# Absolute decay factors and one causal mask in a retention kernel, parameters spread by matmuls, and another written-out order of its first half

## The chip, the cores and the metric

One core of one Trainium2 chip runs the whole program. The time is the device time of one execution, in microseconds; for the kernel before it is the median of three runs.

## The reference, cut to what matters

Three layers in a row. First a retention layer over q, k, v of shape (2, 8, 768, 64): a state of 64x64 per head decays by gamma at each position.

```python
gamma = 1.0 - 2.0 ** (-5.0 - np.arange(H, dtype=np.float32))
for t in range(S):
    state = gamma[None, :, None, None] * state + np.einsum('bhd,bhe->bhde', k[:, :, t], v[:, :, t])
    y[:, :, t] = scale * np.einsum('bhd,bhde->bhe', q[:, :, t], state)
```

Its output, as 1536 tokens of 512 features, passes two feed-forward layers of 2048 hidden units. The first has a rational function between its two products (parameters a, four numbers, and b, two numbers); the second has h * sigmoid(h).

```python
P = a[0] + a[1] * h + a[2] * h2 + a[3] * h3
Q = 1.0 + np.abs(b[0]) * np.abs(h) + np.abs(b[1]) * h2
g = P / (Q + 1e-06)
```

The weights of the feed-forward layers arrive as 64-bit floats.

## The kernel before, in words

**Retention by chunks.** The sequence is cut in 6 chunks of 128 positions for each of 2 batches: 12 chunks c0 to c11, chunk index ci = c // 2. The function `attention(c, ...)` loads four tiles of 256 KB each: qT and kT (features down the partitions), vn and kn (positions down the partitions); kn is missing for the last ci. TensorE makes the scores (`sc`, L458, 16 instructions, into two PSUM banks). VectorE multiplies them with a mask that holds the decay between two positions of one chunk (`am` tiles, two instructions, the 512 KB tile `msk`). kn is multiplied with gamma to the minus position (`gk`, in the small tile `cst`). From kn and vn TensorE makes what the state grows by (`grow`, L491, 16 instructions), and from vn and the masked scores, with the old state `bd` and the scaled q, the output (`outs`, L503 x16 and, from the second ci on, L513 x8). q is multiplied with gamma to the position (tile `gq`, one load of 256 KB for each ci above 0) after its scores are made, since the scores take it plain. ScalarE and VectorE split the output in a high and a low part (`xh`, `xl`), the operands of the feed-forward layer. The kn and q multiplications are VectorE's in chunks 0 to 3 and GpSimd's (POOL) after that. Chunks 0 to 3 make up the first group of 512 tokens, 4 to 7 the second.

**Feed-forward.** The weights come in pairs of 128-wide blocks; a use u of a pair has four raw loads of 512 KB ("in" 0 and 1, "out" 0 and 1). ScalarE (two ACTIVATEs) and VectorE (one instruction) turn a raw load into fp32, ScalarE makes the high part and POOL the low part (L414). A use has two steps; step s has an input product of 12 matmuls (L550, into PSUM bank h0 or h1 in the first 20 steps), some ten elementwise instructions of ScalarE and VectorE, a split in `gh` and `gl`, and four output products of 3 to 6 matmuls (L603, banks acc0 to acc3). The first two input products need chunks 0 to 3 and the weights of use 0; the third (step 2) needs use 1.

**Buffers that gate loads.** Three buffers each for qT, kn, vn and for raw weights, two for kT: the load of kT of c2 waits until the scores of c0 are made, and a raw load until the merge of the raw load three before it. All loads are issued by SyncE (SP), one queue, in order: a load that waits holds back those behind it.

**The order.** The program is a list of 2312 operations; the packed constant `ORDER` gives their places, and each engine runs its operations in that order. Nothing is moved at run time. Unpacked, SP's list begins like this (q0 is qT of chunk 0; u0.in1 the second "in" load of use 0; spill a store of converted weights):

```
q0 k'0 cst msk u0.out0 v0 k0 k'1 q1 k1 u0.in0 q2 k'2 v1 gq2 k'3 q3 u0.in1 v2 k2 k3 q4 k'4 v3 k4 gq4 a v4 k5
u0.out1 b u1.in0 u1.in1 spill q5 k'5 v5 u1.out0 k7 k6 spill k'6 q6 v6 gq6 ...     (k' is kT, k is kn)
```

and TensorE's:

```
warm-up, sc0, outs0, sc1, grow0, sc2, outs1, sc3, grow1, outs2, grow2, sc4, outs3, grow3, grow4, outs4,
step 1 in, step 0 in, sc5, grow5, outs5, sc6, grow6, outs6, step 2 in, sc7, step 0 out ...
```

The tile `par` holds the parameters; two loads spread a and b over the 128 partitions, VectorE negates a (L354), ScalarE takes the absolute values of b (L828, L829). A warm-up of 11 products of zeros (L837) runs at the start.

Of the kernel before, what the change touches and what calls it, by code (L numbers as in the profile page):

```python
# [23 lines left out]
R = {'lw': -463.92, 'T0': 689.59, 'tau0': 13.93, 'tau1': 122.19, 'c0': -129.63, 'dc': 67.51, 'conv': 39.61, 'half': 427.29, 'absl': -34.77, 'raw': 455.03, 'ret': 752.06, 'spl': -417.39, 'hi': 301.24, 'lo': 31.56, 'inn': -277.93, 'later': -32.81, 'split': -554.53, 'out': 359.39, 'evac': -363.13, 'qload': -20.08, 'scl': 238.79, 'sc': 858.37, 'am': -44.15, 'gr': 112.48, 'av': -547.62, 'bd': 198.47, 'xh': -201.14, 'xl': 110.32, 'glp': 48, 'lop1': 24, 'lop2': 30, 'scp': 4, 'ps': 17, 'ksc': 103.89, 'qa': -467.29, 'ka': 0, 'late': 20, 'mid': 4, 'pev': -317.29, 'pld': -385.01, 'cg': -489.85, 'wm': 11, 'mk': 26.43, 'ck': 21.3, 'g2': (1, 0, 2), 'ch0': 269.21, 'ch1': -102.81, 'ch2': 64.3, 'ch3': 22.33, 'ch4': -52.46, 'ch5': 5.42, 'ch6': -78.23, 'ch7': 237.84, 'ch8': 90.06, 'ch9': -61.88, 'ch10': -106.39, 'ch11': -212.52, 'ru0': 218.22, 'lu0': -107.8, 'ru1': 40.68, 'lu1': -106.06, 'ru2': 91.09, 'lu2': 146.01, 'ru3': -37.17, 'lu3': -39.51, 'rhalf': 125.38, 'wsum': 20.0, 'kd': 4, 'hb': 20}  # L24
# [7 lines left out]
    'c-jru0~-+L8UWDO@0VM)wrp!*aoNVQ?G_f6ZQHiBY}>Z6g{`{xSDfcWgQ$Q2a15fu50D5F0|P+>hzyY+BE*DP5F27ZTu2UaAPO9Z6L1oe!cIsJ=^',  # L32
    'zPYgM5%5_Cp592n8TBB!FG88<Ign_z_aT9!LpUAv<J&c(51ZLmEg6r=buOhF{<($OJjzAf$rSZ~$_^At(X`ArIt*BTyPj!Ou_@DuF;5s0(L7;Xh#',
    'f3(CVjI0NONG8~0^Pz*}Kc{m5TAU70+3Qz?qLRF{%-{310hZ68B7*vA`P!p=dcW_V)AovWP!waYlwV)0}#9q)E4nqrQ39X<5{D7z63S5J$fN1y<U',
    'PEN855GY}AZ!D@p%FBI#?S+P#*5GsuER~Z1x=tS+<<1#93o-B+i(Y7K@@xgZ{ZzWf|wWs+d@0I3+>?^+=urN0XxEF=medi8$`ngP!J1XEbIbZp*z',
    'IG_?Q4cKq2e{MG>$xI*x(gAu3LV;qW*71I6(n^n;HO9TQ_hOoYWS36{mASO)vTAMg|&!4pV_8L$LChJWER^oLLI1qMJl%#6QaGE9!YVtR~&m2e6S',
    'g&|NFdt+=Ih{Iqy6v0v$7b{>Dtc)ozBmRgrF$-43fshFYL00?;|AfIX60%_}tc}?*2j;}S*avgrAp8?YLp`j6^>GyZfpu{(4#$#M9v8znTnbgG8Z',
    'LopkP=70Sjdg3FfF#i*7zH?!8AAyQe#_ekNvR$HpKBT0XkqioCMWzD0ajV*a`DvUd)GiZ~)GLiZ~1>!$g<~jj%CJ#m+b$o8U;CfYWd~&W0}76}w?',
    'm?2a{X4lKu&xB^GvM4Sb)a0brA**FKAV>4`lbD<^n#Cfm=SK(Tmi}P?kF2Do08rR`uT#p-YBhH6ScnQZ~HCl)Zp*k&q8ng&D<3T)xNAWNo!{2ckj',
    'K=j)n^r;t+5nSq2=>Eu(2S<w7F>jv@d_Tn<5-94(kd8>jpzh6q!!eiuHy>0fmd-k)T5Jl3QuEWYDw4dCf>px*bA57VqA)=VFzx-C%6o6;~l(<XK*',  # L40
    'KO!<zIIpJRPm1NZP5zQC9G3fIC}tVQ?nH~NDA;lKD5zvDUFjpuPMKE#bMmUiKGoJo`EHNL@bxCh74J{(VP5$GKvy+@+WFo7=MMQla0XexccEzp|&',
# [93 lines left out]
def retention_two_mlps(  # L135
# [114 lines left out]


    cst = Buf("cst", [P, NGAM])
    msk = Buf("msk", [P, 2, HP, P])
    gk = cst.t[:].rearrange("p (c h) -> p c h", h=H)
    par = Buf("par", [P, 14])
    ab, na, b1, b0, lb = par.t[:, 0:6], par.t[:, 6:10], par.t[:, 10:11], par.t[:, 12:13], par.t[:, 13:14]
    cq = par.t[:, 11:12]
# [61 lines left out]
    def heads(t):  # L319
        return t[:].rearrange("p (a t) -> p a t", a=HP)  # L320
# [103 lines left out]
    def attention(c, s_banks, o_banks):  # L424
# [10 lines left out]
        kT, qT = load(0.0, kTs, kt[b, ci]), load(0.1, qTs, qt[b, ci])  # L435
        vn = load(0.3, vns, v[b, ci])
        kn = load(0.4, kns, k[b, ci]) if grows else None
        if grows:

            if c < R["ka"]:  # L440

# [498 lines left out]
```

## Time and profile before

| | us |
|---|---|
| three runs | 580.83, 581.77, 584.45 (median 581.77) |
| profiled execution, device time | 583.26 |
| its span, first to last instruction | 581.5 |
| TensorE busy in the span | 567.3 |
| VectorE, ScalarE, POOL busy | 427.6, 405.2, 174.2 |

The profiled execution lies 1.49 us above the median of the three runs; 1.76 us of it are outside the span. Busy times overlap; they add up to more than the span.

### The profile page before, as it was taken

How to read it: one execution, taken by the hardware profiler on the slowest of the kernel's cores; microseconds unless marked ns; L12 is line 12 of the kernel's file. 1: busy time of each engine (PE TensorE's matmuls, PEld its weight loads, DVE VectorE, ACT ScalarE, POOL GpSimd, SP SyncE). 2: the span in 40 equal slices, each digit the busy share in tenths (PEclk: the TensorE clock that was granted, in tenths of full speed). 3: DMA queues.
4: the chain of work that ended last, by engine and by line, in shares of the span. 5: the costliest groups of instructions: out<-in, count | busy, mean ns of one | idle time of the engine just before them, and what ended most of it. 6: DMA issues, size and time to landing. Idle time of an engine off the chain costs nothing.

```text
span 581.5 us, 8229 instructions
## 1 busy us (share of the span) xinstructions
PE 567.3 (98%) x2902; PEld 467.4 (80%) x2902; DVE 427.6 (74%) x673; ACT 405.2 (70%) x697; POOL 174.2 (30%) x141
## 2 busy tenths in 40 slices
PE   7879999999999999999999999999999999999997
PEld 6767777888888888888888888888888888888885
DVE  3878888798788887798878566578887888663331
ACT  2577988999988887787998888776634545334432
POOL 0435545534644523553463653310000000000000
PEclk8997999999999999999999999999999999999999
DMA  8999856443123310032044667865433422116811
GB/s 299 304 386 312 276 165 235 144 144 112 36 76 106 104 42 20 0 92 90 19 162 147 217 218 246 280 212 167 139 98 108 146 73 91 54 38 207 278 57 73
DMA packets 42585, 86.81 MB, mean 149 GB/s; under 512 B 4656, under 2 KB 4656, under 8 KB 42544
## 3 DMA queue, kind: packets, MB, share of 16 engines
q1 hardware_dynamic: 42544, 86.29, 44.5%
q8 instruction: 23, 0.38, 0.3%
q14 instruction: 18, 0.15, 0.1%
HBM read 65.30 MB, written 20.97 MB: 148 GB/s over the span
## 4 chain that ended last, share of the span: by engine, by line
PE 92%; DMA 3%; ACT 1%; issue 1%; DVE 1%; SPq 1%; POOL 1%; POOLq 0%; DVEq 0%; ACTq 0%
PE acc L603 45%; PE h L550 19%; PE a L550 10%; PE h L766 7%; PE a L766 7%; DMA raw<-in_moe_w_in_dram 2%; PE a L513 1%; DMA qT<-in_qt_dram 1%; PE a L503 1%; PE a L458 1%; SPq L362 1%; PE a L491 1%; PE acc L458 0%; POOL kn L336 0%; ACT wt L328 0%
## 5 line engine op out<-in xcount | busy, mean ns | idle before, releaser
L336 POOL TENSOR_TENSOR gl<-s,gh 128x512 fp32r<-128x512 f32 x48 | 62.7, 1307 | 111.6 <-ACT gh L328 74.8
L603 PE MATMUL acc<-gh,oh 128*128 128x512 f32 x192 | 75.8, 395 | 0.0
L603 PE MATMUL acc<-gl,oh 128*128 128x512 f32 x192 | 74.8, 390 | 0.0
L603 PE MATMUL acc<-gh,ol 128*128 128x512 f32 x192 | 74.8, 389 | 0.0
L603 PE MATMUL acc<-oh,gh 128*128 128x512 f32 x192 | 74.7, 389 | 0.0
L603 PE MATMUL acc<-oh,gl 128*128 128x512 f32 x192 | 74.7, 389 | 0.0
L603 PE MATMUL acc<-ol,gh 128*128 128x512 f32 x192 | 74.7, 389 | 0.0
L550 PE MATMUL h<-xh,ih 128*128 128x512 f32 x168 | 66.3, 395 | 0.0
L550 PE MATMUL h<-xh,il 128*128 128x512 f32 x168 | 65.7, 391 | 0.0
L550 PE MATMUL h<-xl,ih 128*128 128x512 f32 x168 | 65.7, 391 | 0.0
L414 POOL TENSOR_TENSOR il<-wt,ih 128x512 fp32r<-128x512 f32 x36 | 47.1, 1317 | 48.4 <-ACT ih L409 46.2
L343 DVE SCALAR_TENSOR_TENSOR wt<-wt,raw 128x512 int32<-128x512 int32 x64 | 46.2, 732 | 19.9 <-ACT raw L328 12.4
L414 POOL TENSOR_TENSOR ol<-wt,oh 128x512 fp32r<-128x512 f32 x36 | 47.6, 1325 | 29.0 <-ACT oh L409 24.5
L328 ACT ACTIVATE raw<-raw,par 128x512 int32<-128x512 uint32 x64 | 48.3, 759 | 6.1 <-DMA raw<-in_moe_w_in_dram 5.0
L343 DVE SCALAR_TENSOR_TENSOR s<-s,par,h 128x512 f32<-128x512 f32 x65 | 48.2, 744 | 1.2
L328 ACT ACTIVATE wt<-raw 128x512 f32<-128x512 f32 x64 | 42.2, 660 | 6.4 <-DMA raw<-in_moe_w_out_dram 4.0
L603 PEld LDWEIGHTS acc<-gh,oh 128*128 128x128 f32 x192 | 36.0, 188 | 7.8
L603 PEld LDWEIGHTS acc<-oh,gh 128*128 128x128 f32 x192 | 36.0, 188 | 7.5
L603 PEld LDWEIGHTS acc<-gl,oh 128*128 128x128 f32 x192 | 36.0, 188 | 7.5
L603 PEld LDWEIGHTS acc<-oh,gl 128*128 128x128 f32 x192 | 36.0, 188 | 7.5
L603 PEld LDWEIGHTS acc<-ol,gh 128*128 128x128 f32 x192 | 36.0, 188 | 7.4
L328 ACT ACTIVATE gh<-s 128x512 fp32r<-128x512 f32 x56 | 35.0, 626 | 9.9 <-PE acc L603 3.7
(249 smaller groups left out, 1292.0 us busy)
## 6 DMA issues: line engine op xcount, KB each, us to landing
raw<-in_moe_w_out_dram SPq DMA_DIRECT2D x32, 512.0 KB, 4.4
raw<-in_moe_w_in_dram SPq DMA_DIRECT2D x32, 512.0 KB, 4.7
spill<-wt SPq DMA_DIRECT2D x48, 256.0 KB, 4.7
wt<-spill SPq DMA_DIRECT2D x48, 256.0 KB, 2.9
qT<-in_qt_dram SPq DMA_DIRECT2D x12, 256.0 KB, 5.7
kT<-in_kt_dram SPq DMA_DIRECT2D x12, 256.0 KB, 5.9
vn<-in_v_dram SPq DMA_DIRECT2D x12, 256.0 KB, 5.9
kn<-in_k_dram SPq DMA_DIRECT2D x10, 256.0 KB, 6.1
```

What stands on the lines that cost most here:

```text
L328: lambda: nc.scalar.activation(out=out_, in_=in_, func=func, **kw),
L336: op(eng, dur, rank, lambda: e.tensor_tensor(out=out_, in0=in0, in1=in1, op=alu), reads, writes, port)
L343: lambda: nc.vector.scalar_tensor_tensor(out=out_, in0=in0, scalar=scalar, in1=in1, op0=op0, op1=op1),
L362: op("swdge" if swdge else "sync", us, rank, lambda: e.dma_start(out=out_, in_=in_), reads, writes)
L414: e.tensor_tensor(out=sl.t[nm + "l"][:, us], in0=wt.t, in1=sl.t[nm + "h"][:, us].bitcast(F32), op=ALU.subtract)
L458: nc.tensor.matmul(heads(sb_[j].t)[:, hp, :], kT.t[js, hp, :], qT.t[js, hp, :], start=True, stop=True)
L491: nc.tensor.matmul(st.t[j * D : (j + 1) * D, hp * D : (hp + 1) * D], kn.t[:, 2 * hp + j, :], vn.t[:, 2 * hp + j, :], start=(hp == 0), stop ...
L503: nc.tensor.matmul(heads(xo.t)[j * D : (j + 1) * D, hp, :], vn.t[:, 2 * hp + j, :], heads(am[j].t)[:, hp, :], start=(hp == 0), stop=not mo ...
L513: nc.tensor.matmul(heads(xo.t)[:, hp, :], old.t[:, hp, :], qT.t[:, hp, :], start=False, stop=True, skip_group_check=True,)
L550: nc.tensor.matmul(h.t, sl.t[w][:, ws], x[g].t[:, c, :], start=(n == 0), stop=(n == 3 * KD - 1))
L603: nc.tensor.matmul(a.t, a1, a2, start=(first and n == 0), stop=(last and n == 2))
L766: nc.tensor.matmul(b_.t, w[0](c, wlo), x[0](c, xlo), start=(start and n == 0), stop=(n == 5), skip_group_check=True)
```

## The change

- The mask no longer holds decays. A tile `causal` (128x128, zeros and ones) is made on chip by VectorE from 128 more columns of `cst`; it is read for all four heads of a score bank by a broadcast. `msk` and its 512 KB load are gone.
- q is multiplied with gamma to the position in every chunk, those of ci 0 too, and now before the scores. For ci 0 the factors are not loaded as a tile: two rows of 2 KB go to two elementwise buffers, and two matmuls with a row of ones (`spread`) write them into PSUM bank acc3, which VectorE reads.
- vn is multiplied with gamma to the minus position in all 12 chunks, in place of kn in 10. Both `grow` and `outs` use the scaled vn.
- a and b come in two loads to one partition (`pin`); one matmul with ones (`params`) spreads them into acc2, from where the negation and the absolute values read.
- An identity tile `ident` is made by two small VectorE instructions; the branch that would use it (`turned`) is off, since `R["turned"]` is empty.
- `ORDER` is another list, of 2323 operations (11 more: 4 multiplications in the chunks, 7 in the preparation). From step 30 of TensorE on, and from like places on the other engines, both lists are the same.

Unpacked, SP's new list begins (row is a 2 KB row, cst+ has the 128 columns more):

```
q0 q1 v1 row row k'0 cst+ v0 a k'1 v2 b gq2 k0 q2 k'2 gq4 q3 q4 k1 k'3 u0.in0 k2 v3 k'4 u0.in1 v4 k4 k3
u0.out0 q5 u0.out1 k'5 u1.in0 v5 u1.in1 spill gq6 k5 q6 k'6 spill v6 k6 u1.out0 u2.in0 u1.out1 q7 ...
```

TensorE's:

```
warm-up, spread, sc0, sc1, grow0, params, outs0, sc2, outs1, grow1, sc3, outs2, grow2, sc4, outs3, grow3, grow4, outs4,
step 1 in, sc5, step 0 in, outs5, grow5, sc6, grow6, outs6, step 2 in, step 0 out (2 of 4), step 3 in, sc7 ...
```

VectorE's, after the memsets (q*, v* are the multiplications, am0 and am1 the masked scores, merge the instruction that joins a raw load):

```
causal, q*0, v*0, q*1, v*1, am1 c0, v*2, am0 c0, negate, am1 c1, ident, q*2, am0 c1, xl0, q*3, am0 c2, am1 c2, xl1,
am0 c3, am1 c3, v*3, merge u0.in0, xl2, bd2, am0 c4, bd2, am1 c4, merge u0.in1, bd3, xl3, merge u0.out0, bd4, xl4, bd4, bd3,
merge u0.out1, step 1, am1 c5, am0 c5, step 1, merge u1.in0, merge u1.in1, step 0 (2), bd5, xl5, bd5, step 0, step 1, am0 c6, am1 c6 ...
```

and POOL's, after its two memsets: q*4, v*4, low u0.in0, low u0.in1, q*5, low u0.out0, v*5, q*6, v*6, low u1.in0, low u1.in1, gl of step 0 ...

The core of the diff:

```diff
+        gam = gk[:, ci, :].unsqueeze(2).to_broadcast([P, H, D])
+        tt("dve" if c < R["kd"] else "pool", rank - R["ksc"], vn.t, vn.t, gam, ALU.mult, [cst], [vn], bcast=True)
+        if more:
+            gq = shared[ci] if ci in shared else load(0.5, gqs, decays[ci - 1])
+            shared[ci] = gq
+            up = gq.t[:]
+        else:
+            gq = bank["acc3"]
+            up = heads(gq.t)
+        tt("dve" if c < R["scp"] else "pool", rank - R["scl"], qT.t[:], qT.t[:], up, ALU.mult, [gq], [qT], port=more)
...
-                msk.t[:, j, :, :],
+                causal.t[:].unsqueeze(1).to_broadcast([P, HP, P]),
                 ALU.mult,
-                [sb_[j], msk],
+                [sb_[j], causal],
...
-        if more:
-
-            gq = shared[ci] if ci in shared else load(0.5, gqs, decays[ci - 1])
-            shared[ci] = gq
-            eng = "dve" if c < R["scp"] else "pool"
-            tt(eng, rank - R["scl"], qT.t[:], qT.t[:], gq.t[:], ALU.mult, [gq], [qT])
...
-    dma(R["mk"], 1.32, msk.t[:].rearrange("p j a t -> p (j a t)"), consts[:, NGAM:], [], [msk])
-    dma(R["ck"], 0.2, cst.t, consts[:, 0:NGAM], [], [cst])
+    rows2 = ew["t"].bufs
+    for j in range(2):
+        dma(-60.0 + j, 0.02, rows2[j].t[0:1, :], consts[0:1, NGAM + j * HP * P : NGAM + (j + 1) * HP * P], [], [rows2[j]])
+    dma(-59.0, 0.25, cst.t, consts[:, 0 : NGAM + P], [], [cst])
+    pa, pb = Cell(), Cell()
+    dma(-58.0, 0.01, pin.t[:, 0:4], moe_a.unsqueeze(0), [], [pa])
+    dma(-57.0, 0.01, pin.t[:, 4:6], moe_b.unsqueeze(0), [], [pb])
...
-    dma(2.0, 0.1, ab[:, 0:4], moe_a.unsqueeze(0).to_broadcast([P, 4]), [], [par])
-    dma(2.0, 0.1, ab[:, 4:6], moe_b.unsqueeze(0).to_broadcast([P, 2]), [], [par])
...
+    first = cst.t[:, NGAM : NGAM + P]
+    op("dve", 0.15, -48.0, lambda: nc.vector.tensor_scalar(out=causal.t, in0=first, scalar1=0.0, scalar2=None, op0=ALU.is_gt, op1=ALU.bypass), [cst], [causal])
...
+    def spread():
+        for j in range(2):
+            nc.tensor.matmul(bank["acc3"].t[j * D : (j + 1) * D, :], ones.t[:, 0:D], rows2[j].t[0:1, :], start=True, stop=True)
+
+    def params():
+        nc.tensor.matmul(bank["acc2"].t[:, 0:6], ones.t, pin.t, start=True, stop=True)
```

## Rows read from the trace of the kernel before

**Rows 1.** The page: busy time, share and instructions of each engine, and the 40 slices of the span.

```profile
PE 567.3 (98%) x2902; PEld 467.4 (80%) x2902; DVE 427.6 (74%) x673; ACT 405.2 (70%) x697; POOL 174.2 (30%) x141
PE   7879999999999999999999999999999999999997
PEclk8997999999999999999999999999999999999999
```

**Rows 2.** Busy time by stretch: us (instructions) of each engine, granted clock, DMA share, GB/s.

```profile
35.00:40.00 5.00, 2.93 (x45) 2.33 (x46) 3.83 (x7) 4.26 (x8) 2.50 (x3) 1.00 1.05 405
40.00:45.00 5.00, 3.28 (x36) 2.54 (x30) 4.68 (x9) 3.92 (x7) 3.60 (x5) 0.97 1.02 376
45.00:50.00 5.00, 4.75 (x40) 4.26 (x41) 3.87 (x7) 3.10 (x6) 2.52 (x2) 0.50 0.70 240
100.00:130.00 30.00, 30.00 (x183) 24.22 (x183) 25.00 (x40) 28.80 (x50) 12.35 (x10) 1.00 0.41 134
```

**Rows 3.** The chain that ended last: start us, us, what; six of its pieces.

```profile
4.78 7.23 DMA qT<-in_qt_dram
...
15.01 5.22 DMA raw<-in_moe_w_in_dram
...
50.35 3.36 PE h L550 x12
...
57.06 2.72 PE h L550 x12
...
65.05 1.09 PE a L513 x8
...
522.57 54.41 PE acc L603 x240
```

**Rows 4.** Issue of the mask's load (start, us), and its KB and us to landing.

```profile
2.12 0.43 SPq L362 DMA_DIRECT2D msk<-in_consts_dram  x1
...
msk<-in_consts_dram SPq DMA_DIRECT2D x1, 512.0 KB, 4.9
```

**Rows 5.** Timeline of TensorE to 54 us: start, us, what [idle before <-releaser].

```profile
1.45 5.06 PE L837 MATMUL h<-u 128*128 128x128 f32 x22 [1.45 <-DVE par L840]
...
21.03 1.10 PE L503 MATMUL h<-am,vn 128*64 128x128 f32 x16 [1.26 <-DMA vn<-in_v_dram]
...
29.94 0.48 PE L550 MATMUL h<-xh,ih 128*128 128x512 f32 x1
...
36.26 1.16 PE L458 MATMUL a<-qT,kT 64*128 64x128 f32 x16 [0.58 <-DMA kT<-in_kt_dram]
...
38.91 0.69 PE L491 MATMUL a<-vn,kn 128*64 128x64 f32 x16 [1.49 <-POOL qT L336]
...
43.31 1.16 PE L458 MATMUL a<-qT,kT 64*128 64x128 f32 x14 [0.24 <-DVE xl L336]
...
46.37 1.97 PE L503 MATMUL a<-am,vn 128*64 128x128 f32 x16
```

**Rows 6.** Timeline of VectorE and POOL, 7 to 24 us: multiplications alone and side by side.

```profile
7.96 1.29 DVE L336 TENSOR_TENSOR am<-a,msk 128x512 f32<-128x512 f32 x2 [6.54 <-PE a L458]
...
16.87 1.27 POOL L414 TENSOR_TENSOR il<-wt,ih 128x512 fp32r<-128x512 f32 x1 [15.15 <-ACT ih L409]
...
17.29 1.40 DVE L336 TENSOR_TENSOR qT<-qT,gq 128x512 f32<-128x512 f32 x1
...
23.02 0.69 DVE L336 TENSOR_TENSOR qT<-qT,gq 128x512 f32<-128x512 f32 x1
```

**Rows 7.** Chunk 7's q: its issue, its us to landing, its scores, and POOL's scaling.

```profile
41.30 0.33 SPq L362 DMA_DIRECT2D qT<-in_qt_dram  x1
...
qT<-in_qt_dram SPq DMA_DIRECT2D x1, 256.0 KB, 6.6
...
53.63 1.16 PE L458 MATMUL a<-qT,kT 64*128 64x128 f32 x16
54.97 1.31 POOL L336 TENSOR_TENSOR qT<-qT,gq 128x512 f32<-128x512 f32 x1 [1.57 <-issue]
```

More of the change, by code (lines that the diff above doesn't have):

```diff
@@ L23 @@
 UNIT = 512
[L24 removed]
+R = {'lw': -463.92, 'T0': 689.59, 'tau0': 13.93, 'tau1': 122.19, 'c0': -129.63, 'dc': 67.51, 'conv': 39.61, 'half': 427.29, 'absl': -34.77, 'raw': 455.03, 'ret': 752.06, 'spl': -417.39, 'hi': 301.24, 'lo': 31.56, 'inn': -277.93, 'later': -32.81, 'split': -554.53, 'out': 359.39, 'evac': -363.13, 'qload': -20.08, 'scl': 238.79, 'sc': 858.37, 'am': -44.15, 'gr': 112.48, 'av': -547.62, 'bd': 198.47, 'xh': -201.14, 'xl': 110.32, 'glp': 48, 'lop1': 24, 'lop2': 30, 'scp': 4, 'ps': 17, 'ksc': 103.89, 'qa': -467.29, 'ka': 0, 'late': 20, 'mid': 4, 'pev': -317.29, 'pld': -385.01, 'cg': -489.85, 'wm': 11, 'mk': 26.43, 'ck': 21.3, 'g2': (1, 0, 2), 'ch0': 269.21, 'ch1': -102.81, 'ch2': 64.3, 'ch3': 22.33, 'ch4': -52.46, 'ch5': 5.42, 'ch6': -78.23, 'ch7': 237.84, 'ch8': 90.06, 'ch9': -61.88, 'ch10': -106.39, 'ch11': -212.52, 'ru0': 218.22, 'lu0': -107.8, 'ru1': 40.68, 'lu1': -106.06, 'ru2': 91.09, 'lu2': 146.01, 'ru3': -37.17, 'lu3': -39.51, 'rhalf': 125.38, 'wsum': 20.0, 'kd': 4, 'hb': 20, 'turned': ()}
 L_SCALE = 2.0**-29 * (1.0 - 2.0**-16)
@@ L37 @@
[L37 to L41, printed above, removed]
@@ new lines @@
+    'WfC^9wib7rZ0Zv1CI02QRK3s%)a28I&d8i1N;4(CW2GAI)z!hi+7oZ8;fTm!04Q@emXaqN*61<0hpcUMPXm}hx!gX+L4Q=5*^n?g(1D~J;M8dn!6',
+    '}mtSjE*t!0X&3r&<!3zOK1<B;0bhxcF+MjLr3@kPa!V$g3_1-dqZse7ka?2@ED#!ABcic@j3hlS0N7eh0kyYeufwD7sSUeFbMvJe$XG{;Y&z>U*Q',
+    '{6#K9052LRwN@CpV(B20y4@gAhcG?*5XVmeHSZ{Zz$hv_i`CdM+D2b19tKpY17FfR^=*N_p*VGXQ|nXn*M!hpZQ?=TJuVSX%+v2ZNBfhw38CqWjh',
+    'hV^kMj0eG5m=zf-U;(U&!*MPo$Lcr&M#CTQJr+j7k)W6jCqr!<1u3u@j)Cl01dCz|Oo>0>PuLu%KwX>wQ(+>E#s=6Bd*Gii9g1N~?1_!AHRi;s*b',
+    '7_XH0X_eF*p8>v!D+ChPki}w#DLD0>|LbI0tgzA2=50K}no}lW+#ihH*F&XF@yN3GJ~1E`$mABX-0^uo(JaKkSdAa3Yq%`Pc;O;VkTg18^p;fnRV',
@@ L249, in at_chunk @@
         return R[f"ch{c}"] + (5.5 * c if c < CPG else T0 + R["c0"] + R["dc"] * (c - CPG))
[L252 to L257, printed above, removed]
+    cst = Buf("cst", [P, NGAM + P])
+    causal, ident = Buf("causal", [P, P]), Buf("ident", [P, P])
+    gk = cst.t[:, 0:NGAM].rearrange("p (c h) -> p c h", h=H)
+    pin = Buf("pin", [1, 6])
+    ones = Buf("ones", [1, P])
+    par = Buf("par", [P, 8])
+    na, b1, b0, lb = par.t[:, 0:4], par.t[:, 4:5], par.t[:, 5:6], par.t[:, 6:7]
+    cq = par.t[:, 7:8]
     cqc, lbc, table = Cell(), Cell(), Cell()
@@ L433, in load, with turn @@
             return buf
-        kT, qT = load(0.0, kTs, kt[b, ci]), load(0.1, qTs, qt[b, ci])
+        sb_ = [bank[x] for x in s_banks]
+        turned = c in TURNED
+        kT = kTs() if turned else load(0.0, kTs, kt[b, ci])
+        qT = load(0.1, qTs, qt[b, ci])
         vn = load(0.3, vns, v[b, ci])
         kn = load(0.4, kns, k[b, ci]) if grows else None
-        if grows:
-            if c < R["ka"]:
-                def decayed():
-                    for n in range(H):
-                        nc.scalar.activation(out=kn.t[:, n, :], in_=kn.t[:, n, :], func=AF.Copy, scale=gk[:, ci, n : n + 1])
-                op("act", 1.95, rank - R["ksc"], decayed, [cst], [kn])
-            else:
-                gam = gk[:, ci, :].unsqueeze(2).to_broadcast([P, H, D])
-                tt("dve" if c < R["kd"] else "pool", rank - R["ksc"], kn.t, kn.t, gam, ALU.mult, [cst], [kn], bcast=True)
-        sb_ = [bank[x] for x in s_banks]
+        if turned:
+            def turn():
+                for hp in range(HP):
+                    nc.tensor.transpose(heads(sb_[1].t)[:, hp, :], kn.t[:, 2 * hp : 2 * hp + 2, :].rearrange("p j d -> p (j d)"), ident.t)
+            op("pe", 1.09, rank + R["sc"], turn, [kn, ident], [sb_[1]])
+            act(rank + R["sc"], kT.t[:].rearrange("p a t -> p (a t)"), sb_[1].t, AF.Copy, [sb_[1]], [kT], True)
+        gam = gk[:, ci, :].unsqueeze(2).to_broadcast([P, H, D])
[8 more added lines that the diff above has]
+        tt("dve" if c < R["scp"] else "pool", rank - R["scl"], qT.t[:], qT.t[:], up, ALU.mult, [gq], [qT], port=more)
         def sc():
@@ L829, in retention_two_mlps @@
-    op("act", 0.1, 15.0, lambda: nc.scalar.activation(out=b0, in_=ab[:, 4:5], func=AF.Abs), [], [par])
+    op("dve", 0.1, -50.0, lambda: nc.vector.memset(ones.t, 1.0), [], [ones])
+    first = cst.t[:, NGAM : NGAM + P]
+    op("dve", 0.15, -48.0, lambda: nc.vector.tensor_scalar(out=causal.t, in0=first, scalar1=0.0, scalar2=None, op0=ALU.is_gt, op1=ALU.bypass), [cst], [causal])
+    op("dve", 0.06, -47.0, lambda: nc.vector.tensor_copy(out=ident.t[:, 0:1], in_=causal.t[:, 0:1]), [causal], [ident])
@@ new lines, in retention_two_mlps @@
+    op("dve", 0.2, -46.0, lambda: nc.vector.tensor_tensor(out=ident.t[:, 1:P], in0=causal.t[:, 1:P], in1=causal.t[:, 0 : P - 1], op=ALU.subtract), [causal], [ident])
+    def spread():
[3 more added lines that the diff above has]
+        nc.tensor.matmul(bank["acc2"].t[:, 0:6], ones.t, pin.t, start=True, stop=True)
+    op("pe", 0.9, -45.0, spread, [ones, *rows2], [bank["acc3"]])
@@ L832, in retention_two_mlps @@
+    op("pe", 0.2, -44.0, params, [ones, pa, pb], [bank["acc2"]])
+    ab = bank["acc2"].t
+    op("dve", 0.06, 15.0, lambda: nc.vector.tensor_scalar(out=na, in0=ab[:, 0:4], scalar1=-1.0, scalar2=None, op0=ALU.mult, op1=ALU.bypass), [bank["acc2"]], [par])
+    op("act", 0.1, 15.0, lambda: nc.scalar.activation(out=b1, in_=ab[:, 5:6], func=AF.Abs), [bank["acc2"]], [par])
+    op("act", 0.1, 15.0, lambda: nc.scalar.activation(out=b0, in_=ab[:, 4:5], func=AF.Abs), [bank["acc2"]], [par])
     warm = ew["u2"].bufs[0]
```

80 lines of the change are left out of this document (39 added, 41 removed).

## The prediction

> **What bounds the kernel now.** I read the page first: TensorE is busy 98% of the span, and only the first three of its 40 slices (14.5 us each) and the last show less than nine tenths; its clock is below nine tenths in the first and the fourth [rows 1]. Then the chain that ended last: its pieces are TensorE's almost without a break from the input product of step 2 on, which ends at 50.35 + 3.36 = 53.71 us, to the last piece [rows 3]. So from 53.7 us on the time is TensorE's work, of which the change takes nothing away, and the one place to win is what lies ahead of it. There the stretches show waste: 6.2 of 10 us busy from 35 to 45, and from 45 to 50 the granted clock is 0.50, the lower of the two levels (1.2 GHz), after that slack [rows 2]. One input product costs 3.36 us there against 2.72 at full clock [rows 3]. The first loads and VectorE set the pace before that: the first output of chunk 2 waited for v2 until 21.03, and at 36.26 and 38.91 TensorE waited for k'5 and for the work on chunk 5 [rows 5].
>
> So I ask one thing: when does the input product of step 2 end with the new list? The same products stand ahead of it in both lists (seven scores, grows and outputs, the inputs of steps 0 and 1), so the difference goes straight to the end, unless something later stalls.
>
> **Loads.** I count 256 KB as one unit. Before, four units and cst have landed at 2.12 + 4.9 = 7.0 us [rows 4], the tenth (q1) at 4.78 + 7.23 = 12.0, the 21st (u0.in1) at 15.01 + 5.22 = 20.2 [rows 3]: 0.83 us a unit, then 0.75. The new list drops the two units of msk and puts the raw loads behind the chunks' tiles. In the same measure (cst+ is 0.34 units) v0, unit 5.3, lands at 8.1; k0 at 11.4; q2 12.2; k'2 13.0; q3 14.5; k1 16.0; k'3 16.7; v3 19.7; u0.in1 22.0; k3, unit 26.3, at 24.2; k'5 28.7; u1.in1, unit 37.3, at 32.5; k6 38.5. A raw load waits for the merge of the one three before it (u1.in1 for u0.out0, about 28 us), which these times allow. The rows of 2 KB and the parameters cost SP an issue each, 0.43 as other loads take [rows 4]; SP is ahead of the transfers there, so I book nothing; without that cover it is 1.7 us.
>
> **Stretch 1, to the input of step 1.** Warm-up ends at 1.45 + 5.06 = 6.5 [rows 5]. `spread` has no row. Nearest are the 12 products of 512 columns in 2.72 us, 0.23 each [rows 3]; eight score products show as 16 instructions [rows 5], so two plain fp32 products may be four: 0.9 us, between 0.45 and 1.8 (half clock). I take 0.9: 7.4. `causal`, `ident` and the negation work on 128, 128 and 4 columns; each is bounded by the 0.69 of 512 [rows 6] and by nothing; together 0.4 on VectorE after 7.4. The multiplication with the factors in PSUM has no row either; am reads its scores from PSUM at 1.29 for two [rows 6], so 0.65, and the mask read by a broadcast I cost like the tile. From 7.4 VectorE then works without a pause: 14 instructions of 0.65 up to am1 of c2 and those 0.4 make 16.9. No load listed above comes later than its turn but k1 and k'3: grow1 from 16.0, sc3 from 16.7, so the output of c2 starts at 17.8 (before 21.03). The scores of c2 write over acc2 and acc3, so they now wait for ScalarE's absolute values of b, behind grow0: about 12.7, a microsecond before q2 is scaled. Then outputs of 2.2 us (1.1 for L503 and 1.09 for L513), grows of 0.69, scores of 1.1 [rows 3, 5]: 17.8 + 2.2 + 0.7 + 1.1 + 2.2 = 24.0, k3 at 24.2, two grows 25.6, the output of c4 27.7. Before, step 1 began at 29.94 [rows 5]: **-2.2 us**.
>
> **Stretch 2, to the scores of c6.** Step 1 to 30.4, the scores of c5 (k'5 is there, POOL has scaled q5 by about 28) to 31.5, step 0 to 34.2, which covers the masking of c5; the old list had nothing to put there and waited 0.58 and 1.49 [rows 5]. Output and grow of c5 to 37.1; the scores of c6 use the same two banks and wait for the split of c5 and VectorE's instructions around it, 36.4 + 0.6 + 2 x 0.65 = 38.3. That is 10.6 us from the start of step 1; before it was 43.31 - 29.94 = 13.4 [rows 5]: **-2.8 us**. VectorE has 17 full instructions between the merge of u0.out1 and am1 of c6, 11 us, and 13 to do them in.
>
> **Stretch 3, to the end of step 2's input.** Scores 1.1, one mask 0.65, the grow, the output 2.2, the product 2.72: 7.4 us with waits, to 45.7. Before, it was 53.71 - 43.31 = 10.4, since the output ran at half clock (1.97 for the part that takes 1.1) and the product too [rows 3, 5]: **-3.0 us**. I take it that the clock stays up, with 2.4 idle us from 35 to 45 in place of 3.8 [rows 2]; if not, up to 2.9 of this is lost.
>
> The sum is -8.0. Off it goes what two engines cost each other. A VectorE multiplication with both inputs in SBUF took 1.40 beside a POOL instruction and 0.69 alone [rows 6]: 0.71 each time. About eight such (q*3, v*3 and six merges) lie on the path between 15 and 40 us, where POOL is now busier with q and v of chunks 4 to 6; I take two meetings, 1.4 us, between none and 5.7. That leaves **-6.6 us**. The two more multiplications for POOL and VectorE each lie beside other work. From step 30 on all lists are the same, and the last 54.41 us [rows 3] don't change.
>
> The Trainium skill ("SBUF — State Buffer", section "Who interferes with whom") says that VectorE with two SBUF inputs and a reading GpSimd exclude each other for a whole instruction, whichever starts second. The row of 1.40, which ends 0.55 after POOL's, agrees; by that rule, taken for all eight, the sum would be the rival's below.
>
> **Rivals.**
> 1. *VectorE and POOL hold each other up* at all eight: -8.0 + 5.7 = -2.3, 579.5. For: the 1.40 [rows 6], and scaling moved ahead of the scores. Against: am, xl and the first two q* read PSUM, and am beside POOL kept its pace. Chance 0.11.
> 2. *ScalarE gives it back.* It is busy 28.80 of 30 us from 100 to 130 [rows 2], and the new list lets it begin conversions later (the first raw load is 22nd, not fifth). If it can't keep a start that is 8 us earlier, TensorE waits in chunks 7 to 11's stretch; half the gain is gone, 578.5. Against: from 35 to 45 it still had 1.8 of 10 us free [rows 2]. Chance 0.14.
> 3. *Slower.* The scaling of q stands ahead of the scores, on POOL from c4 on, behind low parts; TensorE, full from 46 us, waits for it in c7 to c11. One scaling and one instruction ahead of it are 2 x 1.31 = 2.6 us [rows 7], five times 13, so 13 - 6.6 = +6.4: 588.2. It decides where a q lands less than 2.6 us before TensorE comes to its scores. Before, q7 landed at 41.30 + 6.6 = 47.9 and its scores ran at 53.63 [rows 7], 5.7 us; an earlier TensorE eats into that. Chance 0.12.
> 4. *More*: no meetings, VectorE at its 0.6 start to start in the first stretch: -9.5, 572.3. Chance 0.08.
>
> That the change doesn't do what it says can be in one way: SP's list can't speed up a queue that is full; then the loads are as late as before but for the mask's two units, 1.5 us. The unit count above (37.3 against 37 units to u1.in1, k3 at 26 instead of 24, but v3 at 20 instead of 27) says that it is the sequence of the tiles that helps, so I fold this into rival 2.
>
> **How the numbers follow.** The profiled execution would go from 583.26 to 576.7; the median of the runs shown lies 1.49 lower, so 581.77 - 6.6 = **575.2**. The forecast's chance is 0.55, with its own range of 573 to 578 (the clock, meetings, `spread`). The range to 8 in 10 takes in rivals 1 and 2 and half of 4, not 3: 571.5 to 582.5. One per cent is 5.8 us, about what a measurement of this kernel can tell from no change: faster means under 575.95. Of the forecast some six tenths lie there, 0.34, and rival 4: 0.42. Slower by over 1% is two thirds of rival 3: 0.08. The rest, 0.50, is within.
>
> **What would show it.** Stretch 1: the first output of c2 near 17.8, the first L550 near 27.7. Stretch 2: no wait for POOL's q scaling or k'5 at c5, scores of c6 near 38.3. Stretch 3: clock 1.0 from 40 to 50 and step 2's product of 2.72 ending near 45.7. Rival 1: merges and v* of 1.3 or more beside POOL. Rival 2: idle TensorE ahead of L550 or L603 between 55 and 160 on ScalarE; rival 3: ahead of L458 on POOL's q. I am wrong where TensorE's idle time behind 46 us is more than 2 us, or where step 2 ends after 50.

## The result: 1% slower, and the profile after

The changed kernel takes **587.93 us** (median of 7 runs, 586.15 to 588.62) against 580.83 (580.32 to 584.45, 7 runs): ratio 1.0096, 95% interval 1.0070 to 1.0121. I had forecast 575.2, with a range from 571.5 to 582.5.

The profiled execution of after (586.15 us, span 584.3) is 1.8 us under its median, that of before (583.26) 2.4 above, so the two traces show 2.9 of the 7.1 us. Before's longer executions mostly go with a lower granted clock: in one comparison of 18 (that of e9 below), the three with a mean granted clock of 0.999 or 1.000 took 579.36 to 580.16 us, the five at 0.987 to 0.991 582.02 to 585.48; one at 0.997 took 582.47, so the clock isn't all of it.

The page of after: engine totals, two rows of the 40 slices, and the shares of the chain that ended last.

```profile
PE 568.2 (97%) x2908; PEld 464.4 (79%) x2908; DVE 436.2 (75%) x679; ACT 405.4 (69%) x697; POOL 179.9 (31%) x143
PE   8989999899999999999999999999999999999997
PEclk8999999999999999999999999999999999999999
...
PE 77%; ACT 10%; DVE 9%; DMA 2%; issue 1%; SPq 0%; ACTq 0%; DVEq 0%
```

The low clock in the fourth slice is gone [rows 1], but TensorE's busy share now dips in the eighth (102 to 117 us), where before had no dip, and ScalarE and VectorE hold 19% of the chain, which before was TensorE's from 50 us on [rows 3].

The same stretches as [rows 2] in after, and the next one:

```profile
35.00:40.00 5.00, 3.40 (x51) 3.00 (x52) 4.50 (x9) 3.57 (x6) 2.32 (x2) 1.00 1.02 388
40.00:45.00 5.00, 4.02 (x53) 3.43 (x51) 4.49 (x9) 4.80 (x9) 2.52 (x2) 1.00 0.96 360
45.00:50.00 5.00, 5.00 (x23) 4.09 (x22) 4.90 (x8) 4.62 (x8) 4.46 (x4) 1.00 0.64 210
100.00:130.00 30.00, 26.97 (x156) 21.10 (x155) 23.17 (x35) 27.55 (x48) 10.66 (x9) 1.00 0.28 93
130.00:160.00 30.00, 29.04 (x125) 22.53 (x124) 24.20 (x33) 24.35 (x41) 15.55 (x12) 1.00 0.30 110
```

Up to 50 us everything went as I had hoped: more work done, clock 1.00 where it had been 0.50. From 100 to 130, where TensorE had been busy all the time, 3.0 us are idle, and ScalarE is *less* busy than before (27.55 against 28.80): it waits.

TensorE's timeline in after, the rows that answer [rows 5]. In order, they are the first matmul of c2's output, of step 1's input, of c6's scores and of step 2's input, the last matmul of step 2's input, and the first of step 10's and of step 30's input:

```profile
18.82 1.09 PE L505 MATMUL h<-am,vn 128*64 128x128 f32 x16 [0.62 <-DVE xl L338]
...
28.00 0.48 PE L552 MATMUL h<-xh,ih 128*128 128x512 f32 x1
...
39.39 1.16 PE L468 MATMUL a<-qT,kT 64*128 64x128 f32 x16 [1.60 <-issue]
...
44.26 0.47 PE L552 MATMUL h<-xh,ih 128*128 128x512 f32 x1
...
46.84 0.39 PE L552 MATMUL h<-xh,il 128*128 128x512 f32 x1
...
106.01 0.50 PE L552 MATMUL h<-xh,ih 128*128 128x512 f32 x1 [1.07 <-DVE s L345]
...
216.84 0.39 PE L552 MATMUL a<-xh,ih 128*128 128x512 f32 x1
```

The first matmuls of step 2's and step 30's input in before:

```profile
50.00 0.77 PE L550 MATMUL h<-xh,ih 128*128 128x512 f32 x1
...
214.31 0.40 PE L550 MATMUL a<-xh,ih 128*128 128x512 f32 x1
```

Between these two points both lists have the same products of TensorE, so the time between them measures how a list keeps TensorE fed: 164.3 us before, **172.6 after** (before's holds 0.6 us of half clock, 3.36 against 2.72 at step 2's input [rows 3]). A lead of 5.7 us at step 2's start (6.5 at its end, 47.2 against 53.71 [rows 3]) has become a lag of 2.5, and it stays: the last piece of the chain, 54.41 us long, begins at 525.32 against 522.57 [rows 3].

What TensorE waited for from 46 to 500 us, and what ScalarE waited for from 50 to 200, in after (us in all, times, longest):

```profile
PE h L552 <- DVE s L345: 5.3, 9, 1.2
PE a L505 <- issue: 0.3, 1, 0.3
PE acc L605 <- POOL gl L338: 0.2, 1, 0.2
```

```profile
ACT s L330 <- DVE u L345: 7.2, 5, 3.3
ACT gh L330 <- DVE s L345: 3.1, 4, 1.4
ACT ih L411 <- DVE wt L345: 2.2, 2, 1.9
```

Before has this second list too; the same pair stands far down in it:

```profile
ACT s L328 <- DVE u L343: 0.3, 1, 0.3
```

Nothing in the algorithm makes `s` wait for `u`: in `step`, ScalarE's first `s` and VectorE's `u` both only read h (`u` also w). But h is one PSUM bank. The chain of after where it happens first at length, in step 9 (start us, us, what):

```profile
96.92 0.75 DVE s L345
97.67 0.66 DVE u L345
98.33 0.60 DVE am L338
98.93 0.88 DVE wt L345
99.81 0.67 DVE u L345
100.56 0.78 ACT s L330
```

And ScalarE's timeline there:

```profile
96.58 0.68 ACT L330 ACTIVATE w<-h,par 128x512 f32<-128x512 f32 x1
100.56 0.78 ACT L330 ACTIVATE s<-h,par 128x512 f32<-128x512 f32 x1 [3.30 <-DVE u L345]
```

ScalarE is done with step 9's w at 97.26 and stands still for 3.30 us, until VectorE, behind the `u` of step 8, a mask and a merge, has done the `u` of step 9, which reads the same bank. Everything queued on ScalarE stands behind it. The Trainium skill ("PSUM — Partial Sum Buffer", section "PSUM bank collisions raise a hardware error") says that the compiler's scheduler adds a dependency between any two instructions of different engines that touch the same bank and quadrant of partitions, reads included; this wait of a read for a read agrees. Up to step 20 `u` stands ahead of `s` in the new list in steps 6, 7, 9, 14, 16 and 17, in the old one in 10 and 15.

### The profile page after: what moved, and what is told of

Its sections match the earlier page's. It is cut to its first block, busy times and chain, and to the rows that moved or that the text cites. A ratio compares the mean times of both kernels' runs of the same rounds, so it can differ in the third digit from the quotient of the medians.

```text
span 584.3 us, 8254 instructions
## 1 busy us (share of the span) xinstructions
PE 568.2 (97%) x2908; PEld 464.4 (79%) x2908; DVE 436.2 (75%) x679; ACT 405.4 (69%) x697; POOL 179.9 (31%) x143
## 4 chain that ended last, share of the span: by engine, by line
PE 77%; ACT 10%; DVE 9%; DMA 2%; issue 1%; SPq 0%; ACTq 0%; DVEq 0%
PE acc L605 38%; PE h L552 12%; PE a L552 9%; PE h L768 7%; PE a L768 7%; ACT h L330 2%; DVE s L345 2%; DVE u L345 2%; ACT s L330 1%; DVE wt L345 1%; DMA vn<-in_v_dram 1%; DVE s L338 1%; ACT w L330 1%; ACT raw L330 1%; DVE h L345 1%
## 5 line engine op out<-in xcount | busy, mean ns | idle before, releaser
L345 DVE SCALAR_TENSOR_TENSOR wt<-wt,raw 128x512 int32<-128x512 int32 x64 | 51.1, 809 | 18.8 <-ACT raw L330 13.1
L416 POOL TENSOR_TENSOR ol<-wt,oh 128x512 fp32r<-128x512 f32 x36 | 48.8, 1362 | 25.1 <-ACT oh L411 20.5
L552 PEld LDWEIGHTS h<-xh,ih 128*128 128x128 f32 x168 | 31.5, 188 | 16.2 <-DVE s L345 8.7
```

What stands on the lines that cost most here:

```text
L345: lambda: nc.vector.scalar_tensor_tensor(out=out_, in0=in0, scalar=scalar, in1=in1, op0=op0, op1=op1),
L416: e.tensor_tensor(out=sl.t[nm + "l"][:, us], in0=wt.t, in1=sl.t[nm + "h"][:, us].bitcast(F32), op=ALU.subtract)
L552: nc.tensor.matmul(h.t, sl.t[w][:, ws], x[g].t[:, c, :], start=(n == 0), stop=(n == 3 * KD - 1))
```

## The experiments

Theories: **A**, the waits at h's bank, made by the order of the list; **B**, VectorE and POOL holding each other up in SBUF (rival 1), called meetings; **C**, ScalarE is full and eats any lead (rival 2); **D**, for e7 alone, transfers hold TensorE when it comes earlier. Each kernel was timed beside the kernel before on the same chip (medians 580.80 to 581.64 there). Line numbers differ by a few between kernels, as the list's text is longer or shorter. The last three columns come from one trace of each kernel.

| kernel | median us | ratio to before, 95% | step 2 starts | step 30 starts | between |
|---|---|---|---|---|---|
| before | | | 50.00 | 214.31 | 164.3 |
| after | 587.93 | 1.0096, 1.0070 to 1.0121 | 44.26 | 216.84 | 172.6 |
| e1_flip | 583.22 | 1.0041, 1.0023 to 1.0058 | 44.05 | 212.58 | 168.5 |
| e4_nomeet | 586.36 | 1.0083, 1.0061 to 1.0104 | 43.77 | 215.07 | 171.3 |
| e8_flip_nomeet | 582.12 | 1.0007, 0.9984 to 1.0030 | 45.32 | 212.26 | 166.9 |
| e11_s_from_sbuf | 582.60 | 1.0009, 0.9983 to 1.0035 | 45.12 | 212.92 | 167.8 |
| e6_list | 586.34 | 1.0089, 1.0059 to 1.0119 | 45.45 | 219.09 | 173.6 |
| e9_replayed | 577.21 | 0.9944, 0.9923 to 0.9965 | 44.53 | 208.61 | 164.1 |
| e10_replayed_start | 579.31 | 0.9965, 0.9945 to 0.9985 | 45.39 | 209.94 | 164.6 |

**e1_flip: `s` ahead of `u` in the six steps.** Place in the list, step 9 as an example:

```diff
-443 w   449 u   452 s      (step 9)
+443 w   449 s   450 u
```

> The changed kernel with one thing turned in six steps (6, 7, 9, 14, 16, 17): ScalarE's scaled copy of h (s) stands ahead of VectorE's u in the list, so that ScalarE no longer waits for VectorE at the bank of h. In the changed kernel's trace these waits leave ScalarE idle for 7.1 us between 80 and 160. Theory A (waits at the bank, made by the order): most of that comes back, 581 to 584 us. Theory B (VectorE and POOL hold each other up, 8.6 us of stretched VectorE instructions in the first 200 us against 1.4 before): the stretches stay, 586 to 588. Theory C (ScalarE and VectorE are full, no order keeps an earlier start): 585 to 588.

583.22, 4.1 us less between steps 2 and 30. On the other engines no instruction changed its turn by this edit, and on ScalarE only the `s` of steps 6 and 16 passed two and one others; in the other four steps nothing changed but which of the two reads waits for the other. ScalarE's waits for `u` at `s` are gone (the first lines of its waits from 50 to 200 us are now):

```profile
ACT gh L329 <- DVE s L344: 3.1, 4, 1.4
ACT h L329 <- DVE s L344: 2.6, 5, 1.0
ACT u L329 <- DVE u L344: 2.3, 6, 0.6
```

So A holds for over half of the loss. Later this execution lost 1.5 us more, at 252 us, where ScalarE waited 3.0 us for a weight's reload (1.0 in before); why that reload came later isn't settled here.

**e2_hybrid: the new list up to the scores of c8, then the old one.**

```diff
-places 0 to 2322: new
+places 0 to 289: new; the rest in the old list's sequence
```

> The changed kernel's arithmetic; the first 290 operations in the new order (up to the scores of chunk 8, at 63 us in its trace, where it leads the kernel before by 5.8 us), the rest in the order of the kernel before. Theory A (the new order's later part loses the lead): the lead is kept, 575 to 577 us. Theory C (ScalarE and VectorE are full): the lead melts, 579 to 582. Theory B (meetings of VectorE and POOL): they depend on how the two orders fall together; 577 to 583.

586.03 (ratio 1.0079, 1.0060 to 1.0098), and it tells little: the seam itself stalls. A low part of step 6's weights stands on POOL behind a scaling of v, and that scaling waited 6.55 us for its load.

```profile
PE h L551 <- POOL il L415: 4.2, 1, 4.2
```

```profile
80.07 1.04 POOL L337 TENSOR_TENSOR vn<-vn,cst 128x512 f32<-128x512 f32 x1 [6.55 <-DMA vn<-in_v_dram]
```

After that stall, which ends at 83.6 us, TensorE doesn't wait again up to 200 us, but little lead is left to lose by then: step 30 begins 0.9 us later than in before.

**e3_oldorder: the new arithmetic in the old list.**

```diff
-places 0 to 2322: new
+old list; the products with ones, causal, ident and the scalings of q and v put in ahead of their readers
```

> The changed kernel's arithmetic with the whole order of the kernel before; the new operations are put in where their inputs are there, q's scaling just ahead of its scores. Theories A and B (the order, not the arithmetic, costs the time): 580 to 584 us, the old start with a few waits for the scaling. If the arithmetic itself (scaling ahead of the scores, four more multiplications) costs: 586 us or more. With theory C: like the kernel before, 580 to 583.

603.34 (1.0376, 1.0352 to 1.0401): the longest of TensorE's waits up to 200 us are these, and the first is for q's scaling, 4.9 us of it once.

```profile
PE a L467 <- DVE qT L337: 5.7, 2, 4.9
PE acc L604 <- POOL gl L337: 4.2, 1, 4.2
PE a L467 <- POOL qT L337: 3.7, 2, 2.5
```

In the old list, with the new operations put in this way, the new arithmetic costs 21.8 us. The waits for q's scaling, all ahead of 60 us, are of rival 3's kind; the new list avoids them from step 2 on.

**e4_nomeet: POOL doesn't read SBUF for the weights' low parts** (which are left out of the result).

```diff
-e.tensor_tensor(out=low, in0=wt.t, in1=high, op=ALU.subtract)
+if on_pool: e.memset(low, 0.0)
+else: e.tensor_tensor(out=low, in0=wt.t, in1=high, op=ALU.subtract)
```

> The changed kernel, but POOL writes zeros as the weights' low parts of the first layer in place of a subtraction, so that it reads nothing for 72 of its instructions (the low parts are left out of the products). Theory B (meetings): VectorE's stretched instructions fall from 8.6 us to 3 or less in the first 200 us and the time to 578 to 582. Theories A and C: VectorE's stretches go too, but the time falls by 2 us at most, 585 to 588.

586.36; 1.3 us less between steps 2 and 30, and the wait of TensorE stays (in after 5.3, 9 times):

```profile
PE h L555 <- DVE s L345: 4.3, 7, 1.2
```

B is a part, and by this run the smaller one. The run has limits: POOL's other work still meets VectorE, so that VectorE's instructions are held up by 4.6 us in all up to 215 us, where it is 8.5 in after (counted above the shortest of the same kind, where over 0.2 us); and a memset took POOL 0.53 us in place of 1.35, so POOL is also done sooner.

**e5_before_u2first: `u` ahead of `s` in the kernel before.**

```diff
-w  s  ...  u      (steps 6, 7, 9, 14, 16, 17 of the old list)
+w  u  s  ...
```

> The kernel before with its own arithmetic and list, only that in steps 6, 7, 9, 14, 16 and 17 the product u on VectorE stands ahead of ScalarE's first s in the list, as in the changed kernel (five instructions of VectorE and three of ScalarE change places). Theory A (ScalarE's s waits for VectorE's u where both read one PSUM bank and u stands first): ScalarE waits for u six times, 0.7 to 3.3 us each; ScalarE had 1.2 us of idle time in 100 to 130 and 1.1 in 130 to 160, so most of it reaches TensorE: span 583.5 to 587 (581.5 before), ratio 1.004 to 1.009, TensorE idle 2 us or more between 80 and 160 where it had none. Rival C (the new list is simply fuller on VectorE and ScalarE, and the order in the bank is incidental): under 0.7 us, ratio 1.000 to 1.001.

591.52 (1.0188, 1.0154 to 1.0221): slower by 10.2 us, twice the most that A expected. ScalarE's waits for `u` from 50 to 200 us are there:

```profile
ACT s L327 <- DVE u L342: 5.5, 6, 1.8
```

And more: from 80 to 100 us TensorE was idle for 4.5 us and its mean granted clock was 0.83, as the window shows. (This execution, of 593.58 us, is the slowest of four; the others took 591.23 to 591.67.)

```profile
80.00:100.00 20.00, 15.47 (x92) 11.77 (x89) 10.20 (x16) 9.14 (x15) 5.09 (x5) 0.83 0.25 77
```

This edit also changed VectorE's own sequence (five instructions), and what that costs by itself can't be told apart here, so only the sign is A's. The clean test is e11.

**e6_list and e7_list_pe: new lists by replay.** I replayed e1_flip's durations with each engine in its order, the waits for data, and the wait between `s` and `u`, and searched for a better sequence; e7 moves TensorE's instructions too.

```diff
-list of e1_flip
+e6: 113 of VectorE's, 169 of ScalarE's, 28 of POOL's instructions elsewhere; e7: 122, 171, 36 and 127 of TensorE's
```

> The arithmetic of the changed kernel and TensorE's and the loads' order of e1_flip; between step 2 and step 38 some of VectorE's, ScalarE's and POOL's instructions have changed places (113, 169 and 28), found by replaying the durations of e1_flip's trace with each engine in its order, each wait for data and the wait between s and u in one bank. Theory A (the lead of the start was lost by the order of the engines behind TensorE, and no engine is full): step 24 begins about 1.8 us earlier than in e1_flip (179.3), step 38 at 255.8 to 256.5 (258.6 in e1_flip, 258.85 before); span 578 to 580, ratio to before 0.993 to 0.998. Rival C (ScalarE and VectorE are full, any lead is eaten): step 24 at 181 or later, span 581 or more, ratio 1.002 or more.

> As e6_list, but TensorE's instructions change places too (127 of 541 between step 2 and step 38). In the replay step 38 begins at 252.4, that is, all of the lead of step 2 (6.4 us) reaches it. Theory A: span 574.5 to 578, ratio 0.987 to 0.995. Rival D (the reloads and other transfers of the stretch 180 to 260 hold TensorE when it comes earlier): step 38 no earlier than 257, span 579.5 or more, with the waits on DMA.

Both are slower: 586.34, and 591.19 (1.0177, 1.0145 to 1.0208). The expectations read as if C and D were right, but the waits are of another kind: from 46 to 500 us none of TensorE's in e7 is for a DMA. In e6, ScalarE's longest from 50 to 200 us:

```profile
ACT w L329 <- DVE s L337: 6.8, 6, 1.7
```

One of them on ScalarE's timeline, VectorE's instruction that it waited for, and the group of the merges (busy us, mean ns):

```profile
51.19 0.69 ACT L329 ACTIVATE w<-h,par 128x512 f32<-128x512 f32 x1 [1.70 <-DVE s L337]
```

```profile
50.49 0.67 DVE L337 TENSOR_TENSOR s<-s,h 128x512 f32<-128x512 f32 x1
```

```profile
L344 DVE SCALAR_TENSOR_TENSOR wt<-wt,raw 128x512 int32<-128x512 int32 x64 | 56.9, 900 | 18.4 <-ACT raw L329 14.2 <-ACT wt L329 4.0
```

Now `w`, which also reads h, waits for VectorE's multiplication `s<-s,h`, which the search had put ahead of it, since I had told it of `s` and `u` alone. Other pairs of reads of one bank wait in the same way. And the merges take 900 ns in the mean, 809 in after and 732 in before; the search knew nothing of meetings either.

**e8_flip_nomeet: the list of e1 with the edit of e4** (low parts left out as there).

```diff
-list of after
+list of e1_flip; POOL's memset as in e4_nomeet
```

> The list of e1_flip and the edit of e4_nomeet: POOL writes zeros in place of subtracting for the low parts of the weights, so that it reads no SBUF there and VectorE is not held up by it (the low parts are missing from the result). Theory B (what is left of the loss in e1_flip is VectorE held up by POOL): the waits of TensorE for VectorE between 50 and 160 (1.1 and 1.7 us in e1_flip) go, span 578 to 579.5, ratio to before 0.993 to 0.997. Theory A with the order alone: under 0.7 us of gain on e1_flip, span 580.6 to 581.3, ratio 1.002 to 1.004.

582.12: 1.6 us less between steps 2 and 30 than e1, between the two expectations (the profiled span was 579.4). How large the part of B is that this edit takes away stays uncertain: e4 and e8 give 1.3 and 1.6 us between the two steps, but 1.8 and 0.3 by when step 30 begins, and 0.8 and 2.0 by the ratios, whose intervals overlap with those of after and e1. By these figures it is about 2 us at most.

**e9_replayed and e10_replayed_start: the search with both rules** (any two reads of one bank by ScalarE and VectorE in the list's order; a VectorE and a POOL operation on SBUF that meet run one after the other). e10 lets the start move too.

```diff
-list of e1_flip
+e9: 96 of VectorE's, 163 of ScalarE's, 29 of POOL's elsewhere, TensorE's and the loads' sequence kept
```

> The arithmetic of the changed kernel, TensorE's and the loads' order of e1_flip; VectorE's, ScalarE's and POOL's instructions between step 2 and step 38 change places (96, 163, 29), found as in e6_list, but the replay now has two rules that the traces of the runs so far show and that of e6_list lacked: every read of a PSUM bank by ScalarE waits for each read of it by VectorE that stands earlier in the list, and the other way round (not s and u alone); and where VectorE's and POOL's two-input operations in SBUF meet, the later one runs on only when the first has ended. With both rules the replay gives the changed kernel 582.0 us to TensorE's last matmul (580.4 in its trace), e1_flip 577.6 (577.4), and this list 575.2. Theory A with B (the lead is lost to these two waits, which the order decides, and to nothing else): no idle TensorE over 1 us in all between 50 and 500, step 24 at 178.5 to 180.5, step 38 at 255 to 257, span 577.5 to 580 (581.5 before), ratio 0.993 to 0.998. Rival C (ScalarE or VectorE is full): step 24 at 182 or later, TensorE idle 3 us or more, span 582 or more, ratio 1.002 or more.

> As e9_replayed, but the instructions of the three engines change places from the start on too (132, 181 and 31 in all); TensorE's and the loads' order stay. The replay gives 574.2 us to TensorE's last matmul, 1.0 us less than for e9_replayed, all of it ahead of step 2. Theory A with B: step 2's input begins 0.5 to 1 us earlier than in e9_replayed, span 576.5 to 579, ratio 0.991 to 0.997. If the start is set by the transfers and not by the order: same as e9_replayed within 0.5 us.

e9 takes **577.21** (576.63 to 578.58), 3.6 us less than before and 10.7 less than after. Its windows behind 50 us:

```profile
50.00:200.00 150.00, 149.72 (x821) 121.65 (x820) 132.27 (x193) 135.59 (x232) 76.82 (x60) 1.00 0.46 154
200.00:500.00 300.00, 300.00 (x1324) 247.93 (x1323) 235.33 (x373) 214.47 (x371) 82.42 (x63) 1.00 0.39 127
```

And the first of ScalarE's waits from 50 to 200:

```profile
ACT s L329 <- PE h L551: 4.3, 6, 1.5
ACT w L329 <- PE h L551: 3.5, 4, 1.4
ACT w L329 <- PE a L551: 2.6, 3, 1.5
```

TensorE is idle for 0.3 us in 150 (5.9 in after), and ScalarE waits for TensorE, as it should when TensorE is the bound. The same instructions on the same engines keep the lead, with ScalarE at 135.6 of 150 us: C is refuted. VectorE's instructions are still held up by POOL, by 5.4 us from 45 to 215 against 5.7 in e1, and TensorE is fed all the same: what a meeting costs depends on where it falls. e10 took 2.1 us more than e9: step 2 begins at 45.39, 0.9 later, where 0.5 to 1 earlier or the same within 0.5 was expected. Its start is set by something that the replay lacks.

**e11_s_from_sbuf: the bank alone.** The list of after, untouched; in the six steps `s` reads other data in SBUF.

```diff
-act(now, s1.t, h.t, AF.Identity, [h, par], [s1], ...)
+if s in (6, 7, 9, 14, 16, 17):
+    act(now, s1.t, xl[g].t[:, 0, :].bitcast(F32), AF.Identity, [*xl[g].all, par], [s1], ...)
+else:
+    act(now, s1.t, h.t, AF.Identity, [h, par], [s1], ...)
```

> The changed kernel with its list untouched; in steps 6, 7, 9, 14, 16 and 17 alone ScalarE's first s reads 512 columns of the input's low part in SBUF in place of the PSUM bank h (so s, and with it the result, has other numbers; no instruction is added or moved). Theory A (what costs is that s and VectorE's u read one bank, u first): the waits of s for u go, and with them about what e1_flip won by the order: TensorE idle 1.5 us or less between 100 and 160 (4.0 in the changed kernel), step 24 at 180 to 182.5 (185.4), span 580 to 582, ratio to before 1.001 to 1.006. Rival (the order of the engines is at fault and the bank incidental, e1_flip won by having s early): as the changed kernel, step 24 at 184.5 or later, span 583.5 or more, ratio 1.008 or more.

582.60: 4.8 us less between steps 2 and 30, with not one instruction moved. No `s` waits for a `u` any more; `w`, which stands ahead of `s` on ScalarE in all six steps, still waits for the product, so `s` isn't let go any earlier than that. Its windows, where after had 26.97 and 29.04:

```profile
100.00:130.00 30.00, 29.31 (x168) 23.48 (x167) 25.17 (x39) 27.13 (x47) 12.74 (x11) 1.00 0.33 105
130.00:160.00 30.00, 29.76 (x130) 23.85 (x130) 26.15 (x37) 27.60 (x46) 14.25 (x12) 1.00 0.27 98
```

So it is reading the same bank that costs these 4 to 5 us, and the order decides who waits.

## Why the prediction was wrong

**Stretches 1 to 3 held in sum.** First output of c2 at 18.82 (17.8 predicted), step 1 at 28.00 (27.7), the scores of c6 at 39.39 (38.3), step 2's input done at about 47.2 (45.7, or 47.1 with the allowance for meetings), clock 1.00 from 35 to 50, no wait that the profile puts down to k'5 or to POOL's q. The stretches gave -1.9, -2.0 and -2.6 us, where I had -2.2, -2.8 and -3.0 (with before's scores of c6 at 43.31, as there; the first two of their 16 instructions ran at 42.59 already). That is 6.5 us ahead of before, where I had -6.6 after the allowance. That it comes out so close is in part luck: in stretch 1 VectorE, which I had at 0.65 us an instruction without a pause, ran at 0.60, but stood still for 1.27 us, waiting for `params`, and lost 0.9 to POOL.

**One term was read from one execution.** Up to 2.9 of stretch 3's -3.0 was the half clock at 45 to 50 us [rows 2]. The profiled execution had a mean clock of 0.990. Those of 0.999 and 1.000 above can't have lost as much there, since 5 us at 0.50 alone take 0.004 off the mean of 581 us, and before's median lies between. So the gain was read from an execution that had more to lose than most, as far as the clocks tell, for no trace of a faster one was taken: e9, whose trace is 6.1 us ahead of before's (575.4 against 581.5), is 3.6 ahead in medians. Even with the lead kept, as in e9, the forecast was 2.0 us too low (577.21).

**The step that failed** is the claim ahead of the stretches: "so the difference goes straight to the end, unless something later stalls." The sum has no term for a later stall, and 8.3 us came. I checked the claim by asking which *work* stands ahead, and which engine is full; I didn't ask in which *sequence* the new list puts instructions on one bank. Of the 8.3 us that the new list takes longer from step 2 to step 30 than the old, 4.1 (by order, e1) to 4.8 (by bank, e11) are `s` waiting for `u` in six steps; 1.3 to 1.6 by the same measure are VectorE and POOL meeting at the weights' low parts (e4, e8; 0.3 to 2.0 by the others). The rest, 2.8 from e8's 166.9 to e9's 164.1, went when the other pairs of reads and the other meetings were put into another sequence at once; how these two divide it wasn't tried and stays open. In before, one line of 0.3 us in ScalarE's waits already showed the pair.

**Rival 1** was right in kind, at 2 us of the time or less, as far as e4 and e8 show. Up to 45 us three of VectorE's instructions were held up, by 2.3 us in all, where I had allowed two and 1.4; eleven more, 6.2 us, came from 45 to 215, where I had looked for none. **Rival 2** named the right place (TensorE idle ahead of L550, between 55 and 160, on ScalarE's side) and the wrong reason: ScalarE wasn't too late or too full, it stood still with work queued; and I put the price at half the gain where it was more than all of it. **Rival 3** gave 588.2, nearly the measured time, by a mechanism that didn't occur: after 46 us no L468 waits for a scaled q in after. e3 shows what it costs when the list doesn't avoid it. My sign, idle behind 46 us of more than 2 us, did come: 5.9 from 50 to 200.

## What to carry to other kernels

A reordered list can cost more than the operations in it: before you carry a lead from the start to the end, list for each PSUM bank who reads it on which engine and in which order, and see whether the first reader is the one that is ready first. Where an engine is idle while its own work is queued, look at the releaser's name: a wait between two reads of one tile is an order, not a need. And don't count on a gain from a low granted clock that you have seen in one execution.

## What the hardware showed that I hadn't expected

Accesses of one PSUM bank by ScalarE and VectorE, reads after reads too, ran one after the other in the list's order (100.56 against 100.46 for the end of `u`; 51.19 against 51.16 in e6). Laid beside the list, the trace of after has 634 accesses that follow one of the other engine at the same bank; none begins before that one has ended.

VectorE's merge, 0.69 alone, beside POOL in after:

```profile
56.20 1.60 DVE L345 SCALAR_TENSOR_TENSOR wt<-wt,raw 128x512 int32<-128x512 int32 x1
...
60.24 1.41 DVE L345 SCALAR_TENSOR_TENSOR wt<-wt,raw 128x512 int32<-128x512 int32 x1
```

```profile
55.99 1.27 POOL L416 TENSOR_TENSOR il<-wt,ih 128x512 fp32r<-128x512 f32 x1 [1.77 <-ACT ih L411]
...
59.80 1.30 POOL L338 TENSOR_TENSOR qT<-qT,gq 128x512 f32<-128x512 f32 x1
```

POOL's two end at 57.26 and 61.10, VectorE's at 57.80 and 61.65, each some 0.55 later, whenever they began; so do all 14 of VectorE's that were held up to 215 us. The other way round, POOL's scaling at 28.69, begun 0.07 after a merge, took 1.78 us in place of 1.3. This fits the later one running on only when the first is done. With this rule and the bank's, the replay gave TensorE's last matmul within 1.6 us of the trace of after (582.0 against 580.4) and within 0.2 of e1_flip's, whose durations it uses. For its own new lists it was less exact: 575.2 against 571.6 in e9's trace and 574.2 against 573.5 in e10's, which it had put ahead of e9.
